# A fused transformer block on one core: normalisation and modulation move off GpSimd, one transposition in place of two, and the order of work made anew

## The chip, the core and the metric

The kernel runs on 1 core of one Trainium2 chip. A core has TensorE (PE: matrix products into PSUM, PEld is its weight load), VectorE (DVE), ScalarE (ACT), GpSimd (POOL) and SyncE (SP, which here issues nearly all DMAs). Each engine runs its own instruction queue in order, and the queues meet at semaphores. The metric is the device time of one execution in microseconds (us); the runs of the kernel before are three.

## What is computed

One block of a transformer in bf16, for a sequence of 2048 rows of width 640:

```python
mod = (_silu(c) @ w_mod).reshape(c.shape[0], 6, 1, -1)   # sa, ca, ga, sb, cb, gb
h = _layernorm(x, axis=-1) * (1 + ca) + sa
x = x + ga * _A_ref(h, A_wqkv, A_wo)      # attention, 32 heads of 20; key within the 256 rows up to the query
h = _layernorm(x, axis=-1) * (1 + cb) + sb
x = x + gb * _B_ref(h, B_w_gate, B_w_up, B_w_down)   # (sigmoid(h Wg) * (h Wu)) Wd, inner width 1536
```

## The kernel before

**Tiling.** The 2048 rows are 8 chunks (`a` = 0 to 7) of 256, each of two blocks of 128. For a chunk the kernel does in turn:

- `ln1` (from line 803): loads x, takes statistics (`ln_stats`, from line 737) and normalises in place; then turns the rows into columns, `hT`, and modulates. Chunks 0 and 1 turn on PE (`pe_transposes`, the evacuation from PSUM modulates, lines 799 and 800). The later ones turn by a DMA transposition (line 770) and are modulated in place (`modulate`, lines 778 and 779).
- `qkv`: products of 5 x 320 columns into PSUM, evacuated by DVE or ACT (lines 825 and 826) into `stg` for Q and K, which are then turned, and into `V`.
- `score_set` and `burst`: 6 sets of scores for each half of the heads (3 in chunk 0), 90 in all. A set fills four banks of PSUM, of which there is one buffer (`S`). ACT takes the exponential (line 937, 1.876 us), GpSimd masks the edges (lines 945 and 947), and PE sums values over a half's sets into two neighbouring banks of `M`.
- `norm`: DVE turns those two banks in blocks of 32 (line 988), takes the reciprocal of the sums (line 993), divides (line 995) and turns back (line 997). Two DMAs by way of a DRAM buffer, `doc`, bring the result into `oT`.
- `outproj`: products with wo, the first residual on DVE (line 1051), statistics, normalisation, DMA transposition and modulation into `h2T`.
- `mlp`: six pairs of gate and up products, tanh on ACT (line 1091), the glu product on DVE (line 1093), then the products with wd and the second residual (line 1112), and the DMA out.

**The normalisation.** For each of two blocks DVE takes two `bn_stats` (line 744) and an aggregation (line 746). GpSimd adds epsilon (line 749) and takes the power -1/2 (line 751), and one product per block makes minus mean times that (line 755). A normalisation is then a product and a sum (line 760), on DVE or on GpSimd. `XHE` names the engines that may take it, `MOE` those that may take a modulation.

**The prologue.** The modulation vector is made from silu(c) and three slabs of w_mod, which lie for that time where wd, wu and `hh` come later. PE multiplies each 128-row piece of the first slab as it lands (`modA`, `mA` is read out at line 732), with idle products between them (`fill`, line 653, and `warm`, line 642). The gates are folded into wo (line 1136) and wd (line 1077), a piece at a time on DVE.

**What sets the order.** No order is written out. `Prog.schedule` (from line 149) is a list planner: every operation has engines that may run it, a duration, a latency to its readers and a priority, and is placed on the engine that can start it first; among those that could start within a small window the priority decides. `PRI` shifts the priority of each kind of operation in each chunk by a number found outside the code. `port=True` marks DVE operations that the planner starts only when GpSimd is done, and the reverse. The order of each engine's queue, SP's too, is fixed by this when the program is built. Large weights (`bulk`) go through `chain`: a load may start when the one `DEEP` places back has landed.

```python
def chain():
    return [bulk[-DEEP]] if len(bulk) >= DEEP else front
```

The planner's `PACE0` and `PACE` give a score set an earliest time; `PE_EPS` is the window for PE.

Of the kernel before, what the change touches and what calls it, by code (L numbers as in the profile page):

```python
# [394 lines left out]
def c_pe(n):  # L395
# [3 lines left out]
PE_EPS = 0.141  # L399
PRI = {  # L400
    "amodu2": 9.3, "amodu3": -8.2, "amodu4": -88.6, "amodu5": -20, "amodu6": 43, "amodu7": 9, "apow0": 48.2,
    "apow1": 20.4, "apow2": 13.1, "apow3": -3.2, "apow4": -9, "apow5": 57.1, "apow6": 6.3, "apow7": 148.9,
    "astats0": -115.9, "astats2": -2.3, "astats3": -6.5, "astats4": 11.9, "astats5": -40.2, "astats6": -7.2,
    "atr2": -17, "atr3": -9.7, "atr4": 39.6, "atr5": 21.5, "atr6": 44.6, "atr7": 42.7, "axh0": 0.8, "axh1": 19.7,
    "axh2": 156.9, "axh3": 2.9, "axh5": -22.8, "axh6": 9.3, "axh7": -54.4, "bmodu0": 126.1, "bmodu1": 40.4,
    "bmodu2": 3.2, "bmodu3": 8.1, "bmodu4": -27.5, "bmodu5": 29.2, "bmodu6": -38.8, "bmodu7": 2.3, "bpow0": -12.3,
    "bpow1": -25.8, "bpow2": -3.6, "bpow3": 2.6, "bpow4": 23.5, "bpow5": -91.8, "bpow6": -2.4, "bpow7": -41.3,
    "bstats0": -27.1, "bstats1": -13.4, "bstats2": 9.8, "bstats3": 7, "bstats4": 2.4, "bstats5": -202.3,
    "bstats6": -1.7, "bstats7": -4.9, "btr0": -21.8, "btr1": -6.8, "btr2": 2.5, "btr3": 47.8, "btr4": 12.3,
    "btr5": -8.3, "btr6": 13.4, "btr7": 2.1, "bxh0": 1.1, "bxh1": -22.1, "bxh2": -2.1, "bxh3": 9.8, "bxh4": 21.6,  # L410
    "bxh6": -16.9, "bxh7": 12, "divide_0": 82.2, "divide_1": -4.7, "divide_2": 15.7, "divide_3": 13.6,
    "divide_4": 10.2, "divide_5": 10.5, "divide_6": 54.8, "down0": 67.2, "down1": 78, "down2": -3.1, "down3": 350.9,
    "down4": 114.6, "down6": 212.6, "down7": 13.6, "evqk0": 52.1, "evqk1": -14.4, "evqk2": 9.4, "evqk3": 13.1,
    "evqk4": 219.1, "evqk5": 50.7, "evqk6": 92.4, "evqk7": 34.6, "evqt0": 12.1, "evqt1": 160.3, "evv0": 3.4,
    "evv1": -5.6, "evv2": -3.9, "evv3": -0.9, "evv4": -6.5, "evv5": -28.9, "evv6": 6.9, "evv7": -3.5, "exp0": 43.9,
    "exp1": -25.4, "exp2": 156.2, "exp3": -15, "exp4": -34.1, "exp5": -28.7, "exp6": 24.3, "exp7": -25.4,
    "glu_0": 6.1, "glu_1": 21.7, "glu_2": 35.5, "glu_3": -16, "glu_4": -47.7, "glu_5": -9.6, "glu_6": -16.2,
    "glu_7": -15.9, "hTe0": -48.9, "hTe1": 0.2, "mask0": 96.8, "mask1": 2.7, "mask2": 33.7, "mask3": -16.3,
    "mask4": 141.5, "mask5": -12, "mask6": 92.1, "mask7": -13.4, "mlpg0": -25, "mlpg1": -24.5, "mlpg2": -24,
    "mlpu0": -25, "mlpu1": -24.5, "mlpu2": -24, "modb": -1, "modc": -0.8, "n_ow_0": -23.2, "n_ow_1": -17.7,  # L420
    "n_ow_2": -11.1, "n_ow_3": -61.2, "n_ow_4": -53.5, "n_ow_6": -3.1, "n_ow_7": -25.8, "oT_0": 33.6, "oT_1": -1.6,
    "oT_2": 14.5, "oT_3": -3.8, "oT_4": 55.9, "oT_6": -0.9, "oT_7": -3.3, "out": 6.8, "projk0": 4.5, "projk1": 12,
    "projk2": 394, "projk3": 157.7, "projk4": 21.4, "projk5": 189, "projk6": 15, "projk7": 7.2, "projq0": -62.7,
    "projq1": -34.6, "projq2": 51.7, "projq3": 33, "projq4": -15, "projq5": -10.5, "projq6": 468.1, "projq7": -7.6,
    "projv0": -30.9, "projv1": 19.1, "projv2": 152.9, "projv3": -2.2, "projv4": 60.2, "projv5": 41.1,
    "projv6": 285.1, "projv7": 183.7, "ptr0": -566.3, "ptr1": -245.2, "pv0": 18.7, "pv1": -2.9, "pv2": -12.3,
    "pv3": 4.1, "pv4": -11.6, "pv5": -18.8, "pv6": -88.2, "pv7": 104.2, "qkt2": 213.9, "qkt3": -6.3, "qkt4": 56.1,
    "qkt5": 18.6, "qkt6": 1.3, "qkt7": 5.8, "qtr0": -59.2, "qtr1": -6.6, "recip_0": 77.8, "recip_1": -10.5,
    "recip_2": 1.6, "recip_3": -88.1, "recip_4": 54.1, "recip_5": -1.7, "recip_6": 22.9, "recip_7": 10.1,
    "res1_0": 2.2, "res1_1": -17.7, "res1_2": -17.2, "res1_3": -20.4, "res1_4": 7, "res1_5": -126.9, "res1_6": -1.7,  # L430
    "res1_7": 45.3, "res2_0": 1.1, "res2_1": -11.9, "res2_2": -31.5, "res2_3": 51.8, "res2_4": 56.6, "res2_5": 0.1,
    "res2_6": -6.3, "res2_7": 58.7, "score0": -340, "score1": 16.4, "score2": -33.9, "score4": -104.9, "score5": -3,
    "score6": 7.3, "score7": -39.7, "tanh_0": -42.8, "tanh_1": -15.8, "tanh_2": 2.7, "tanh_3": -21.7,
    "tanh_4": -19.1, "tanh_5": -8.3, "tanh_6": -10.9, "tanh_7": -37.8, "tr1_0": 4.7, "tr1_1": 6.4, "tr1_2": 25.6,
    "tr1_3": -54, "tr1_4": 33.5, "tr1_5": 26.4, "tr1_6": -24.5, "tr2_0": 18.5, "tr2_1": -10.4, "tr2_3": -15.8,
    "tr2_4": -48.9, "tr2_5": 3.9, "tr2_7": -18.1, "wd": 0.6, "wds": -30.7, "wg": 27.5, "wm1": 26.4, "wm2": 15.6,
    "wo": -3.8, "wo0": 118.2, "wo1": 11.2, "wo2": 256.4, "wo3": 110.2, "wo4": 70, "wo5": 62.6, "wo6": -58.9,
    "wo7": 84.2, "wos": 7.1, "wu": -18.6, "x10": 1524.7, "x11": 1508.2, "x12": 1434.7, "x13": 1422.4, "x14": 1683.5,
    "x15": 1773.4, "x4": 1288, "x5": 929.8, "x6": 122, "x7": 26.3, "x8": 1341.3, "x9": 1354.8, "y0": -7.1,
    "y1": -20.9, "y10": -20.8, "y11": -5.7, "y12": -76.7, "y13": -41.2, "y14": -33.8, "y15": -8, "y2": 14.6,  # L440
    "y3": -5.6, "y4": -2.6, "y5": -11, "y6": -0.7, "y7": 42.2, "y8": -54.6, "y9": -32.1,
}
TR1 = 2
NPH = 2
NPQ = 2
DEEP = 4
MW = 64
PACE0 = 80.17
PACE = -6.665
AFTER = 0  # L450
LEAD = 2
FILL = 2
# [7 lines left out]
XHE = ('dve', 'pool')  # L460
MOE = ("dve", "act", "pool")


def build(nc, A_x, A_wqkv, A_wo, B_x, B_w_gate, B_w_up, B_w_down, c, w_mod, out, S=2048):
# [50 lines left out]
    p_st = sbpool("st", 3, [128, 34], F32)  # L515
# [51 lines left out]
    def load_x(pool, b, prio, tmin=0.0, eng="sp"):  # L567
        t = Tile(pool, f"{pool.name}_{b}")
        dma(lambda: t.ap[:], lambda: x_flat[b * 128:(b + 1) * 128, :], 0.47, writes=[t.r()], prio=prio, tmin=tmin, tag=f"x{b}" if pool is p_x0 else f"y{b}",
            eng=eng, lat=-0.7 if b > 3 else -0.4 if b < 2 else -1.0)  # L570
        return t
# [8 lines left out]
    def load_wm(i, kt, prio, tmin=0.0):  # L580
        if i:
            raise AssertionError
        return dma(lambda: wm_ap[i][:, kt, :], lambda: wm_src[:, kt, i * 1280:(i + 1) * 1280], 1.1, writes=[Rm[i][kt]], prio=prio, tmin=tmin, tag=f"wm{i}",
                   lat=-0.7)
# [15 lines left out]
    def load_w3(k, prio, halves):  # L600
# [6 lines left out]
        if k == "wk" and BQ != "sp":  # L607
            front.append(o)

    x0 = {}  # L610
    x0[0], x0[1] = load_x(p_x0, 0, 0), load_x(p_x0, 1, 0.1)
    for kt in range(NDT):
        load_wm(0, kt, 0.2 + 0.01 * kt)
    load_w3("wq", 0.30, True)
# [580 lines left out]
```

## Time and profile before

| | us |
|---|---|
| runs | 344.87, 343.16, 343.44 (median 343.44) |
| profiled execution | 344.87, its span 343.1, mean granted clock 0.995 |
| exponentials on ACT (line 937) | 168.8 in 90 |
| masks on GpSimd (lines 945, 947) | 78.8 and 68.1 |
| modulation on DVE (line 779) | 8.0 in 13 (hT) and 6.8 in 18 (h2T) |
| modulation on ACT (line 778) | 6.0 in 11 (hT) and 9.3 in 17 (h2T) |
| modulation on GpSimd (line 779) | 3.7 in 6 (hT) and 2.7 in 5 (h2T) |

A row of the profile's groups gives the line, the engine, the operation, what is written and read with its shape, the count, then busy time and mean duration in ns of one, then the engine's idle time just ahead of these instructions and who ended it. In rows of stretches each engine has its busy time and its number of instructions, then the granted clock, the DMA engines' busy share and the rate. PE's busy time counts products whose ends are modelled, so a full stretch may still hold short losses.

### The profile page before, as it was taken

The page shows a single profiled execution, that of the slowest core. Times are in us where ns is not written, and L with a number is a line of the kernel's source. Part 1 is how long each engine was busy: PE and PEld are TensorE (multiplying, and loading weights), DVE is VectorE, ACT ScalarE, POOL GpSimd, SP SyncE. Part 2 cuts the span into 40 slices and gives each one's busy share as a digit, 9 for nine tenths or more (in the row PEclk, how much of TensorE's full clock was granted, in tenths as well). Part 3 has the DMA queues.
Part 4 walks back from the last instruction along what each step waited for, and adds up shares of the span by engine and source line. Part 5 has one row for each costly group of instructions (what it writes and reads, how often), then busy time and mean ns, then how long its engine had stood idle before and what let it go on. Part 6 is the DMA issues. An engine that isn't in the chain of part 4 may idle for free.

```text
span 343.1 us, 10138 instructions
## 1 busy us (share of the span) xinstructions
PE 328.2 (96%) x4142; PEld 232.3 (68%) x4142; DVE 220.6 (64%) x440; ACT 232.2 (68%) x224; POOL 185.4 (54%) x285
## 2 busy tenths in 40 slices
PE   8889699989979999999999999999999999999997
PEld 2557365645756577766668767766676788887885
DVE  5378889498899964636784744558754654637333
ACT  1587669887966879878988877886888672120220
POOL 5044656668864876656797456559947471001000
PEclk9999899999999999999999999999999999999999
DMA  7999926799990391022763093004231211210301
GB/s 227 371 313 313 382 86 121 159 175 171 237 235 10 76 160 44 16 84 72 168 105 70 21 147 97 3 22 72 44 38 42 76 39 40 79 42 10 109 0 39
DMA packets 71688, 38.73 MB, mean 113 GB/s; under 512 B 46682, under 2 KB 68442, under 8 KB 71642
## 3 DMA queue, kind: packets, MB, share of 16 engines
q1 hardware_dynamic: 71632, 38.09, 45.3%
q8 instruction: 32, 0.52, 0.6%
q14 instruction: 14, 0.11, 0.1%
q10 hardware_dynamic: 10, 0.00, 0.0%
HBM read 21.96 MB, written 5.24 MB: 79 GB/s over the span
## 4 chain that ended last, share of the span: by engine, by line
PE 75%; DVE 9%; DMA 5%; SPq 3%; issue 2%; ACT 2%; POOL 2%; DVEq 0%; ACTq 0%
PE M L661 62%; PE S L662 7%; PE M L662 6%; SPq L536 3%; ACT E L937 2%; DMA wv<-in_A_wqkv_dram 2%; DVE wd L1077 2%; DMA wd<-in_B_w_down_dram 2%; DVE hT L779 2%; DMA hT<-x 1%; DVE x L1051 1%; DVE st L744 1%; POOL E L945 1%; POOL E L947 1%; DVE Tn L995 1%
## 5 line engine op out<-in xcount | busy, mean ns | idle before, releaser
L937 ACT ACTIVATE E<-S 128x2048 bf16<-128x2048 f32 x90 | 168.8, 1876 | 34.8 <-PE S L662 34.0
L945 POOL TENSOR_SCALAR_AFFINE_SELECT E<-E 128x512 bf16<-128x512 bf16 (+2 forms) x90 | 78.8, 877 | 79.5 <-ACT E L937 78.1
L947 POOL TENSOR_SCALAR_AFFINE_SELECT E<-E 128x512 bf16<-128x512 bf16 (+1 forms) x84 | 68.1, 812 | 0.0
L661 PE MATMUL M<-h2T,wg 128*128 128x256 bf16 x480 | 62.7, 273 | 2.0 <-DVE hh L1093 1.9
L661 PE MATMUL M<-h2T,wu 128*128 128x256 bf16 x480 | 64.4, 273 | 0.0
L1093 DVE SCALAR_TENSOR_TENSOR hh<-sig,M 128x512 bf16<-128x512 f32 x48 | 32.7, 681 | 47.9 <-PE M L661 33.1
L661 PE MATMUL M<-wd,hh 128*128 128x320 bf16 (+2 forms) x396 | 56.1, 295 | 0.0
L661 PEld LDWEIGHTS M<-h2T,wg 128*128 128x128 bf16 x480 | 45.3, 98 | 10.9 <-issue 2.2
L661 PEld LDWEIGHTS M<-h2T,wu 128*128 128x128 bf16 x480 | 45.2, 98 | 8.6 <-issue 2.7
L1091 ACT ACTIVATE sig<-M 128x512 f32<-128x512 f32 x48 | 28.5, 594 | 31.7 <-PE M L661 28.8
L661 PEld LDWEIGHTS M<-wd,hh 128*128 128x128 bf16 x396 | 37.0, 98 | 15.2 <-issue 1.5
L662 PE MATMUL S<-QT,KT 20*128 20x256 bf16 (+1 forms) x960 | 35.9, 245 | 1.6 <-ACT E L937 1.5
L988 DVE STREAM_TRANSPOSE T<-M 128x512 f32<-128x512 f32 x32 | 21.1, 696 | 20.2 <-PE M L662 20.1
L744 DVE BATCH_NORM_STATS2 st<-x 128x6 f32<-128x320 bf16 x64 | 28.3, 477 | 4.1 <-DMA x<-in_A_x_dram 3.8
L749 POOL TENSOR_SCALAR st<-st 128x2 f32<-128x2 f32 x16 | 4.8, 304 | 47.0 <-DVE st L746 46.4
L662 PEld LDWEIGHTS S<-QT,KT 20*128 20x128 bf16 x960 | 14.1, 92 | 22.3 <-ACT E L937 18.1
L1112 DVE TENSOR_TENSOR x<-M,x 128x320 bf16<-128x320 f32 (+2 forms) x33 | 15.6, 474 | 19.7 <-PE M L661 19.6
L661 PE MATMUL M<-wv,hT 128*128 128x320 bf16 x160 | 27.1, 314 | 1.2 <-DMA wv<-in_A_wqkv_dram 0.9
L661 PE MATMUL M<-wq,hT 128*128 128x320 bf16 x160 | 24.7, 299 | 0.6 <-DVE V L826 0.3
L661 PE MATMUL M<-wo,oT 128*128 128x320 bf16 x160 | 24.6, 300 | 0.5 <-DVE x L1051 0.5
L661 PE MATMUL M<-wk,hT 128*128 128x320 bf16 x160 | 24.8, 300 | 0.1
L662 PE MATMUL M<-E,V 128*32 128x256 bf16 (+1 forms) x960 | 22.7, 246 | 1.5 <-POOL E L947 0.9
(78 smaller groups left out, 334.2 us busy)
## 6 DMA issues: line engine op xcount, KB each, us to landing
x<-in_A_x_dram SPq DMA_DIRECT2D x32, 160.0 KB, 2.4
doc<-On SPq DMA_DIRECT2D x64, 40.0 KB
out_dram<-x SPq DMA_DIRECT2D x15, 160.0 KB
wg<-in_B_w_gate_dram SPq DMA_DIRECT2D x5, 384.0 KB
wu<-in_B_w_up_dram SPq DMA_DIRECT2D x5, 384.0 KB
wd<-in_B_w_down_dram SPq DMA_DIRECT2D x4, 480.0 KB
wd<-in_w_mod_dram SPq DMA_DIRECT2D x5, 320.0 KB, 4.9
wu<-in_w_mod_dram SPq DMA_DIRECT2D x5, 320.0 KB
```

The costliest lines, as they stand in the source:

```text
L536: return e.dma_start(dst(), src())
L661: return e.matmul(o, l, r, start=st, stop=sp, skip_group_check=True)
L662: return e.matmul(o, l, r, start=st, stop=sp, tile_position=tp, skip_group_check=True)
L744: A("dve", lambda e, g, bi=bi, j=j: e.bn_stats(v(bi * 12 + j * 6, 6), src[bi].ap[:, j * 320:(j + 1) * 320]), 0.48, reads=[src[bi].r()], wr ...
L779: return e.tensor_scalar(ap, ap, sc[:, dt:dt + 1], sh[:, dt:dt + 1], op0=ALU.mult, op1=ALU.add)
L937: A("act", lambda e, eng: e.activation(E.ap[:], Sp.ap[:], ACT.Exp, scale=SM_SCALE), 1.876, reads=[Sp.r()], writes=[E.r()], prio=3, tag=f"e ...
L945: return e.affine_select(ap, ap, pattern=[[0, ap.shape[1]], [1, 128]], compare_op=ALU.is_ge, fill=0.0, base=0, channel_multiplier=-1)
L947: return e.affine_select(ap, ap, pattern=[[0, ap.shape[1]], [-1, 128]], compare_op=ALU.is_ge, fill=0.0, base=-1, channel_multiplier=1)
L988: A("dve", lambda e, g, h=h: e.transpose(T1.ap[:, 512 * h:512 * h + 512], X[h].ap), 0.694, reads=[X[h].r()], writes=[T1.r(h)], prio=3.5, t ...
L1091: A("act", lambda e, g, pg=pg, sg=sg: e.activation(sg.ap[:], pg.ap[:], ACT.Tanh, scale=0.5), c_act(512), reads=[pg.r()], writes=[sg.r()], ...
L1093: A("dve", lambda e, g, pu=pu, sg=sg, f0=f0: e.scalar_tensor_tensor(out=hh.ap[:, f0:f0 + 2, :], in0=sg.ap[:].rearrange("p (a b) -> p a b", ...
L1112: A("dve", lambda e, g, ps=ps, bi=bi, c0=c0, n=n: e.tensor_tensor(x1[bi].ap[:, c0:c0 + n], ps.ap[:, 0:n], x1[bi].ap[:, c0:c0 + n], op=ALU. ...
```

## The change

- `TR1` 2 to 1: one transposition of 1024 columns over both banks of `M` in place of two of 512. The code path was there.
- `XHE` without GpSimd: every normalisation on DVE, as subtraction of the mean and a product; the two small products of line 755 are gone.
- `MOE` without GpSimd: modulation on DVE or ACT.
- The first two x blocks are loaded from ACT's queue, in place of the front of SP's.
- silu(c) is spread to 128 columns by one copy in place of two of 64.
- `DEEP` 4 to 3; nine idle products of two in the warm-up in place of five; `FILL` 2 to 1.
- The planner's constants: durations and latencies of DMAs and of DVE operations, `PE_EPS`, `PACE0`, `PACE` and nearly all of `PRI` (left out below). With them the order on all engines is another one. DVE's queue has 441 instructions (440 before), ACT's 229 with two more DMA issues among them (224) and GpSimd's 232 (285).

In that order all five pieces of the first slab are multiplied ahead of the transposes of x, the scalings of wo are spread over more of DVE's queue, and those of wd stand in groups of 3, 4, 1, 2, 1 and 1 between other work. SP's queue has one piece more of the second slab behind wv. The last scores stand, as before, ahead of two chunks of MLP.

```diff
-PE_EPS = 0.141
+PE_EPS = 0.116
...
-TR1 = 2
+TR1 = 1
...
-DEEP = 4
+DEEP = 3
...
-PACE0 = 80.17
-PACE = -6.665
+PACE0 = -178.4
+PACE = -4.513
...
-FILL = 2
+FILL = 1
...
-XHE = ('dve', 'pool')
-MOE = ("dve", "act", "pool")
+XHE = ("dve",)
+MOE = ("dve", "act")
...
-    p_st = sbpool("st", 3, [128, 34], F32)
+    p_st = sbpool("st", 3, [128, 32], F32)
...
-        dma(lambda: t.ap[:], lambda: x_flat[b * 128:(b + 1) * 128, :], 0.47, writes=[t.r()], prio=prio, tmin=tmin, tag=f"x{b}" if pool is p_x0 else f"y{b}",
-            eng=eng, lat=-0.7 if b > 3 else -0.4 if b < 2 else -1.0)
+        dma(lambda: t.ap[:], lambda: x_flat[b * 128:(b + 1) * 128, :], 0.47 if b > 1 else 0.9, writes=[t.r()], prio=prio, tmin=tmin, tag=f"x{b}" if pool is p_x0 else f"y{b}",
+            eng=eng, lat=0.05 if b > 1 else 1.2)
...
-        return dma(lambda: wm_ap[i][:, kt, :], lambda: wm_src[:, kt, i * 1280:(i + 1) * 1280], 1.1, writes=[Rm[i][kt]], prio=prio, tmin=tmin, tag=f"wm{i}",
-                   lat=-0.7)
+        return dma(lambda: wm_ap[i][:, kt, :], lambda: wm_src[:, kt, i * 1280:(i + 1) * 1280], (1.12 - 0.06 * kt if kt < 4 else 1.2), writes=[Rm[i][kt]],
+                   prio=prio, tmin=tmin, tag=f"wm{i}")
...
-                            prio=prio + 0.01 * k, tag=tag, lat={"wm1": -1.0, "wm2": -0.6}.get(tag, 0.05), extra=list(extra) + chain(), eng=BQ,
+                            prio=prio + 0.01 * k, tag=tag, extra=list(extra) + chain(), eng=BQ,
...
-                    (2.35 if hi - lo == 640 else 0.95 if i == 0 else 1.35), lat=-1.0, writes=[R_w3[k][lo // 320]] if halves else R_w3[k], prio=prio, tag=k)
+                    (2.35 if hi - lo == 640 else 1.28), writes=[R_w3[k][lo // 320]] if halves else R_w3[k], prio=prio, tag=k)
...
-    x0[0], x0[1] = load_x(p_x0, 0, 0), load_x(p_x0, 1, 0.1)
+    x0[0], x0[1] = load_x(p_x0, 0, 0, eng="act"), load_x(p_x0, 1, 0, eng="act")
...
-    A("dve", lambda e, g: e.tensor_copy(silubc[:, :, 0:MW], siluc[:].unsqueeze(2).to_broadcast([128, NDT, MW])), 0.45,
-      reads=[R_siluc], writes=[R_silubc], prio=-1)
-    R_silub2 = R("silub2")
-    A("dve", lambda e, g: e.tensor_copy(silubc[:, :, MW:128], siluc[:].unsqueeze(2).to_broadcast([128, NDT, 128 - MW])), 0.45,
-      reads=[R_siluc], writes=[R_silub2], prio=6)
+    A("dve", lambda e, g: e.tensor_copy(silubc[:], siluc[:].unsqueeze(2).to_broadcast([128, NDT, 128])), 0.8,
+      reads=[R_siluc], writes=[R_silubc], prio=0)
...
-    for i in range(5):
+    for i in range(9):
...
-            ops.append(pe_chain(ps, 320, pairs, [[Rm[i][kt], R_silubc, R_silub2] for kt in range(NDT)], prio, "modb"))
+            ops.append(pe_chain(ps, 320, pairs, [[Rm[i][kt], R_silubc] for kt in range(NDT)], prio, "modb"))
...
-            if "pool" in XHE:
-                A("pool", lambda e, g, bi=bi: e.tensor_scalar(st.ap[:, 32 + bi:33 + bi], v(24 + 2 * bi, 1), v(30 + bi, 1), -1.0,
-                                                              op0=ALU.mult, op1=ALU.mult), 0.25,
-                  reads=[st.r("r"), st.r(("m", bi))], writes=[st.r(("n", bi))], prio=1, tag=f"{ln}pow{a}")
-
-                def xh(e, g, bi=bi):
-                    return e.tensor_scalar(dst[bi].ap[:], src[bi].ap[:], v(30 + bi, 1), v(32 + bi, 1), op0=ALU.mult, op1=ALU.add)
-            else:
-                def xh(e, g, bi=bi):
-                    return e.tensor_scalar(dst[bi].ap[:], src[bi].ap[:], v(24 + 2 * bi, 1), v(30 + bi, 1), op0=ALU.subtract,
-                                           op1=ALU.mult)
-            A(XHE, xh, {"dve": 0.5, "pool": 1.2}, port=True,
-              reads=[src[bi].r(), st.r("r"), st.r(("m", bi))] + ([st.r(("n", bi))] if "pool" in XHE else []), writes=[dst[bi].r()], prio=prio - 0.5, tag=f"{ln}xh{a}")
+            A(XHE, lambda e, g, bi=bi: e.tensor_scalar(dst[bi].ap[:], src[bi].ap[:], v(24 + 2 * bi, 1), v(30 + bi, 1),
+                                                       op0=ALU.subtract, op1=ALU.mult), {"dve": 0.44, "pool": 0.95}, port=True,
+              reads=[src[bi].r(), st.r("r"), st.r(("m", bi))], writes=[dst[bi].r()], prio=prio - 0.5, tag=f"{ln}xh{a}")
...
-        return A("sp", fn, dur, reads=reads, writes=writes, prio=prio, work=work, tag=tag, lat=-0.7)
+        return A("sp", fn, dur, reads=reads, writes=writes, prio=prio, work=work, tag=tag)
...
-            A(MOE, mo, {"dve": 0.4, "act": 0.59, "pool": 0.6}, port=True, reads=[dst.r(("t", bi)) for bi in range(2)] + Rmod, writes=[dst.r(dt)],prio=prio, tag=f"{ln}modu{a}")
+            A(MOE, mo, {"dve": 0.34, "act": 0.59, "pool": 0.55}, port=True, reads=[dst.r(("t", bi)) for bi in range(2)] + Rmod, writes=[dst.r(dt)],prio=prio, tag=f"{ln}modu{a}")
...
-                fills.append(fill(FILL, [o]))
+                fills.append(fill(2 * FILL, [o]))
...
-          0.92, port=True, reads=[T1.r(0), T1.r(1), Dr.r()], writes=[Tn.r()], prio=4, tag=f"divide_{a}")
+          0.82, port=True, reads=[T1.r(0), T1.r(1), Dr.r()], writes=[Tn.r()], prio=4, tag=f"divide_{a}")
...
-                    reads=[On.r()], writes=[Rj], prio=1, tag=f"n_ow_{a}", lat=-0.6)
+                    reads=[On.r()], writes=[Rj], prio=1, tag=f"n_ow_{a}")
...
-                0.22 * (t1 - t0), reads=R_doc[0] + (R_doc[1] if q else []), writes=[oT.r(q)], prio=1.5, tag=f"oT_{a}", lat=0.6)
+                0.22 * (t1 - t0), reads=R_doc[0] + (R_doc[1] if q else []), writes=[oT.r(q)], prio=1.5, tag=f"oT_{a}")
```

## The prediction

> **What bounds the kernel now.** I read the busy shares first, then the slices in time, then the PE waits, then the stretches where PE idles, then the groups for prices.
>
> The page's busy shares:
>
> ```profile
> span 343.1 us, 10138 instructions
> PE 328.2 (96%) x4142; PEld 232.3 (68%) x4142; DVE 220.6 (64%) x440; ACT 232.2 (68%) x224; POOL 185.4 (54%) x285
> ```
>
> PE is the bound: only 343.1 - 328.2 = 14.9 us of the span are not PE. The edit takes no projection, score, value or MLP product away, so it can gain at most those 14.9 us, and it loses whatever new PE idleness it makes. By stretches of 10 us (stretch, then busy PE, PEld, DVE, ACT, POOL, then clock, DMA share, GB/s):
>
> ```profile
> 10.00:20.00 10.00, 8.26 (x90) 5.62 (x88) 4.83 (x13) 6.27 (x13) 2.32 (x5) 1.00 1.06 363
> 20.00:30.00 10.00, 9.73 (x112) 6.99 (x108) 7.91 (x21) 8.83 (x14) 3.64 (x6) 1.00 0.97 339
> 30.00:40.00 10.00, 7.24 (x129) 4.68 (x117) 9.29 (x19) 7.45 (x7) 7.09 (x8) 1.00 1.08 324
> ...
> 70.00:80.00 10.00, 8.39 (x90) 5.05 (x89) 9.81 (x23) 8.95 (x11) 6.77 (x11) 1.00 0.89 211
> ...
> 100.00:110.00 10.00, 7.45 (x134) 5.37 (x135) 9.31 (x20) 4.81 (x5) 4.69 (x9) 1.00 0.27 85
> ...
> 160.00:170.00 10.00, 10.00 (x170) 6.57 (x162) 6.14 (x15) 8.81 (x9) 6.88 (x12) 1.00 0.71 159
> ```
>
> Three stages. Up to 30 us the DMA share is about 1: loads set the pace. From 30 to 120 us PE is busy 81.4 of 90 us (8.6 idle) and DVE 78.4 of 90 (0.87; sums of the nine stretches). The three stretches where PE idles most are three of those where DVE is above 0.92. From 120 us PE shows next to no idle time until the end. The PE's waits name the engine (waiter, releaser, total, times, longest):
>
> ```profile
> PE M L661 <- DVE stg L826: 2.9, 2, 2.7
> PE M L661 <- DVE hh L1093: 1.9, 1, 1.9
> ```
>
> The first is at 38.94 us: the evacuation of a K half stands on DVE behind one modulation that took 1.85 us and one scaling of wo that took 1.39 us; their kinds' shortest are 0.33 and 0.49. GpSimd runs three masks, 4.35 us, in just that time. The second is at 102.96 us: a glu product stands behind nine scalings of wd. So DVE in its first third is the second resource, and the change is about DVE. Prices:
>
> ```profile
> L988 DVE STREAM_TRANSPOSE T<-M 128x512 f32<-128x512 f32 x32 | 21.1, 696 | 20.2 <-PE M L662 20.1
> L997 DVE STREAM_TRANSPOSE On<-Tn 128x1024 bf16<-128x1024 bf16 x16 | 19.8, 1236 | 0.2
> L760 DVE TENSOR_SCALAR x<-x,st 128x640 bf16<-128x640 bf16 x22 | 11.4, 542 | 2.7 <-POOL st L755 2.5
> L760 POOL TENSOR_SCALAR x<-x,st 128x640 bf16<-128x640 bf16 x10 | 8.7, 868 | 0.2 <-POOL st L755 0.2
> L755 POOL TENSOR_SCALAR st<-st 128x1 f32<-128x1 f32 x32 | 8.2, 271 | 1.6
> L779 DVE TENSOR_SCALAR hT<-hT,mA 128x256 bf16<-128x256 bf16 x13 | 8.0, 650 | 0.2 <-DMA hT<-x 0.2
> ```
>
> **The change, part by part.**
>
> *Normalisation and modulation.* The instruction order of the changed kernel has 32 normalisations on DVE (22 now) and 41 modulations (31 now), 29 on ACT (28), none on GpSimd; two more evacuations of hT from PSUM stand on DVE and four others fewer. DVE gains 10 x 0.542 + 10 x 0.477 (14.8 us for 31) + 2 x 0.535 = 11.3 us and loses 2 x 0.483 + 0.485 + 0.69 = 2.1. GpSimd loses 8.7 + 8.2 + 6.4 = 23.3 us; it has 46% idle time and its masks end late at one place only, so that frees little. What counts is where it falls. Of the normalisations on GpSimd four start between 30 and 120 us (46.12, 79.75, 107.22, 116.65 us), and four modulations (34.50, 58.98, 87.19, 90.41). There DVE gets 4 x 0.542 + 4 x 0.650 = 4.8 us more. Ends: 0, if all falls into the 90 - 78.4 = 11.6 us that DVE has free, and 4.8 us, if each stands in front of something that PE waits for. I take 0.87 x 4.8 = 4.2 us: the queue runs in order and is occupied 87% of the time, and two of the three worst PE gaps are such cases. The rest falls after 120 us, where DVE is free a third of the time; nothing.
>
> The order also foresees less of this than the trace shows. The code plans 0.34 us for a modulation, 0.44 for a normalisation, 0.82 for the division. The trace has 0.477, 0.542 and 0.946 (15.1 us for 16). That is 41 x 0.137 + 32 x 0.102 + 16 x 0.126 = 10.9 us of DVE not in the plan; with the constants before (0.40, 0.50, 0.92) it was 31 x 0.077 + 22 x 0.042 + 16 x 0.026 = 3.7. It is the reason to stay near the upper end; it is no term of its own.
>
> *Shorter statistics chain.* Two products of 271 ns go on GpSimd, and a normalisation on the chain falls from 868 to 542 ns. The chain of waits passes this once (78.1 to 80.6 us, the last statistics before the first MLP): 2 x 0.27 + 0.33 = 0.9 us. Ends 0 and 0.9 (PE lost a wait of 0.9 us on a GpSimd mask just after it); I take 0.9.
>
> *One transposition.* Two of 512 columns take 1.31 us back to back (timeline, several times); one of 1024 columns is not in the trace, except in bf16 from SBUF (1.236 us). Saved: 0.07 x 16 = 1.2 us of DVE at most. The first PSUM bank comes free some 0.5 us later, but PE has two others and the next scores; DVE waited 20.1 us in total for PE before these, not the reverse. Ends: -1.2 and, as PE's waits name this transposition nowhere, a burst or two, +1.0 us; I take 0.
>
> *Prologue.* The first two x loads leave SP's queue (0.40 + 0.42 us of issue) for ACT's. The modulation weights are issued 0.9 us earlier, and their last product now stands ahead of the transposes of x instead of behind them. PE idled 0.5 us before the fourth and 0.8 us soon after the fifth, so 0 to 1.3 us earlier start of the projections. SP's queue then waits for landings three loads back instead of four. When wv landed, at 18.56 us, before had 3360 KB to go until the third modulation slab (its last load, issued at 27.05 us, takes 4.3 us, thus 31.3 us): 264 KB per us. PE started on that slab at 31.52 us, straight after it, so this landing sets the pace. The new queue has one more 320 KB load behind wv: 320 / 264 = 1.2 us later. Ends: -1.3 (the early start is kept) and +4.2 (the chain of loads is the limit, and 3 in flight instead of 4 stretch 12.7 us by a third). I take +1.2. The early start is worth nothing as long as PE arrives at the slab before its data.
>
> [...]
>
> *The rest.* The copy of silu(c) in one piece of 640 columns (two of 0.36 and 0.34 now) delays the first product by about 0.3 us, but that one waits for its weights anyway; nothing. More idle matmuls in the warm-up stand in idle time, and the clock reads 1.00 after it. The scalings of wd are now spread between glu products instead of nine in a row: that could take the 1.9 us away, but the same loads land late and the queue is in order, so I count nothing and put it into a rival. After 120 us the order is another one, with the same sets between the same amounts of other products; the trace has no price for it: -1 to +2 us, 0 taken. The tail is the same three pieces.
>
> **Sum.** 4.2 - 0.9 + 0 + 1.2 = +4.5 us. The profiled execution took 344.87 us (span 343.1 and 1.8 around it) and becomes 349.4. It is 1.43 us above the median of the runs, 343.44; the prediction for the median is 343.44 + 4.5 = **347.9 us**.
>
> **Rivals.**
>
> 1. *Faster: the new order frees DVE exactly where PE waits.* Place: the K evacuation at 38.9 us and the glu at 103.0 us. The order has wo's scalings split by other work and wd's in groups of 3, 4, 1, 2, 1, 1 between glu products. If both stalls go and the added work fits into DVE's free time, the prologue stays as it is, and the statistics gain stands: 343.44 - 2.7 - 0.9 = 339.8 with the first alone, 337.9 with both. It decides if DVE's added 4.8 us go into its 11.6 free ones. For it: GpSimd does less beside DVE, and normalisations on DVE have a median of 447 ns, far under the mean. Against it: the single ones reach 1357 ns beside masks, and there are more of them. 0.19.
>
> 2. *All hidden.* PE's 328.2 us are untouched and the 4.8 us vanish in slack: 343.4, within 1.7. Before has 8.6 us of idle PE in the stage, which speaks against so exact a cover. 0.17.
>
> 3. *Slower by much:* three loads in flight starve the prologue (+4.2 in place of +1.2) and a second DVE stall of 2.7 us appears where the order is planned too tight: 347.9 + 3.0 + 2.7 = 353.6. 0.20.
>
> That the edit misses its target is excluded: the instruction order shows all normalisations on DVE and 16 transpositions of 1024 columns.
>
> **Chances.** Forecast (345.2 to 350) 0.44; the three rivals 0.19, 0.17, 0.20. About 0.5%, 1.7 us, is what a measurement of this kernel can tell from no change. Faster by more 0.19, within it 0.17, slower 0.64. The range reaches from the first stall of rival 1 to rival 3: 339.8 to 353.6. The forecast's own range is 345.2 to 350.
>
> **What would show it.** Right: PE idle time between 30 and 120 us above 8.6 us, ended by DVE (evacuations, modulations, glu); DVE near 228.6 us in total, GpSimd near 162; PE's first product of the third slab after 32 us; 120 to 320 us full. Wrong: PE idle below 8.6 us there, or a new PE idle stretch after 120 us, which nothing in this sum pays for.

## The result, and the profile after

The changed kernel takes 340.03 us (median of 339.42 to 340.71), the kernel before 343.80 beside it; the ratio is 0.9888, interval 0.9855 to 0.9921. A second series gave 0.9920 (0.9888 to 0.9953). The prediction was 347.9 us: the sign is wrong. The medians here and below take in every execution, while the ratios leave out those that took over 1.5% more than the fastest of the same kernel, among them one of the changed kernel of 822.42 us at a clock of 1.00, whose cause is open.

The profiled execution took 340.71 us. Its page begins as before's did, with the span and the busy shares:

```profile
span 339.0 us, 10076 instructions
PE 327.9 (97%) x4146; PEld 232.4 (69%) x4146; DVE 220.2 (65%) x441; ACT 233.2 (69%) x227; POOL 159.0 (47%) x232
```

PE's busy time is the same within 0.3 us, so 3.8 of the 4.1 us of span are standstill of PE that is gone (14.9 us before, 11.1 now). GpSimd is at 159.0 (foreseen 162). DVE is at 220.2 where 228.6 was foreseen: with 10 normalisations and 10 modulations more it is no busier than before (220.6). The same stretches as shown for before (stretch, PE, PEld, DVE, ACT, POOL, clock, DMA share, GB/s):

```profile
10.00:20.00 10.00, 9.79 (x106) 6.79 (x105) 6.27 (x16) 8.00 (x15) 0.93 (x2) 1.00 0.97 337
20.00:30.00 10.00, 8.66 (x117) 5.18 (x117) 8.06 (x23) 8.16 (x9) 6.21 (x7) 1.00 0.89 296
30.00:40.00 10.00, 7.93 (x125) 5.30 (x118) 7.19 (x13) 6.84 (x9) 4.91 (x4) 1.00 0.97 245
...
70.00:80.00 10.00, 9.18 (x149) 5.83 (x142) 9.45 (x27) 8.32 (x10) 7.99 (x14) 1.00 0.79 144
...
100.00:110.00 10.00, 10.00 (x144) 6.83 (x133) 9.64 (x22) 7.30 (x5) 4.58 (x6) 1.00 0.01 2
...
160.00:170.00 10.00, 10.00 (x157) 6.48 (x155) 8.14 (x20) 8.70 (x8) 7.63 (x12) 1.00 0.38 101
```

From 100 to 110 us PE is full although DVE is still busy 96% of the time: a busy engine is no stall as long as the right instruction comes first in its queue. Over 30 to 120 us PE is busy 85.04 us (81.38 before), DVE 74.24 (78.36), GpSimd 50.94 (60.70), and the granted clock reads 1.00 (0.98). PE's waits, whole span:

```profile
PE M L657 <- DVE stg L812: 1.9, 3, 1.2
PE M L657 <- DMA hh<-in_w_mod_dram: 1.4, 3, 1.0
PE M L658 <- DVE gbc L705: 1.4, 1, 1.4
```

The waits of 2.7 and 1.9 us in one piece are gone; the longest now is 1.4. The prices of DVE's groups moved too:

```profile
L977 DVE STREAM_TRANSPOSE T<-M 128x1024 f32<-128x1024 f32 x16 | 20.0, 1248 | 16.8 <-PE M L658 16.6
L750 DVE TENSOR_SCALAR x<-x,st 128x640 bf16<-128x640 bf16 x32 | 17.2, 569 | 4.0 <-POOL st L747 3.9
L1063 DVE TENSOR_TENSOR wd<-wd,gbc 128x640 bf16<-128x640 bf16 x12 | 6.5, 565 | 0.2
L765 DVE TENSOR_SCALAR hT<-hT,mA 128x256 bf16<-128x256 bf16 x19 | 6.4, 394 | 0.0
```

Ten more normalisations cost 5.8 us (17.2 less 11.4; 5.4 were priced). But a modulation of hT fell from 650 to 394 ns, a scaling of wd from 761 to 565, a division from 946 to 889: together 19 x 0.256 + 12 x 0.196 + 16 x 0.057 = 8.1 us that the prediction's prices, taken from the old trace, did not have.

**Where the time came from.** I set the two traces side by side at equal amounts of PE work done (lag of the changed kernel, an estimate worked out from the starts of PE's products; the kernels do the products in different orders, so it is good to some 0.6 us, and is less exact where a wait begins):

| place in the kernel before, us | lag, us | what lies there |
|---|---|---|
| 18.8 | -1.7 | earlier start; before waits 0.9 for wv |
| 31.8 | +1.4 | third modulation slab |
| 35.2 | +3.4 | values wait for the gate evacuation (1.4 wait) |
| 43.3 | -1.0 | before's K evacuation stall and what follows it |
| 71 | -0.4 | |
| 84 | -2.0 | before's waits for exponentials, x and a mask |
| 106 | -4.3 | before's glu stall behind nine wd scalings |
| end | -4.5 | |

The prologue's early 1.7 us are lost again and more. Most of the gain is made where rival 1 put it: 4.4 us between 35.2 and 43.3 us, 2.3 between 84 and 106, and 1.6 besides between 71 and 84. Of the 4.4 us, 2.0 only make good what the changed kernel has just lost at its own wait (1.4 to 3.4), so some 2.4 stay. The 4.4 are more than the stall of 2.7 itself, because TensorE's clock fell behind it. Rows of the kernel before:

```profile
36.00:38.00 2.00, 0.27 (x2) 0.00 (x0) 2.00 (x2) 1.63 (x1) 2.00 (x2) 1.00 1.03 400
38.00:40.00 2.00, 0.97 (x22) 0.56 (x22) 2.00 (x5) 0.60 (x1) 1.44 (x2) 1.00 1.05 375
40.00:42.00 2.00, 2.00 (x24) 1.09 (x13) 1.52 (x4) 1.75 (x1) 0.00 (x0) 0.55 1.05 411
42.00:44.00 2.00, 2.00 (x11) 1.16 (x10) 1.57 (x5) 0.36 (x2) 1.81 (x1) 0.59 0.86 318
```

PE is busy in the last two rows, at 0.55 and 0.59 of its clock: 2 x 0.45 + 2 x 0.41 = 1.7 us of delay that no row of idle time shows.

### The profile page after: what moved, and what is told of

The parts are those of the page before. It is cut to its first block, busy times and chain, and to the rows that moved or that the text cites. A ratio compares the mean times of both kernels' runs of the same rounds, so it can differ in the third digit from the quotient of the medians.

```text
span 339.0 us, 10076 instructions
## 1 busy us (share of the span) xinstructions
PE 327.9 (97%) x4146; PEld 232.4 (69%) x4146; DVE 220.2 (65%) x441; ACT 233.2 (69%) x227; POOL 159.0 (47%) x232
## 4 chain that ended last, share of the span: by engine, by line
PE 62%; DVE 0%; issue 0%
PE M L657 52%; PE S L658 5%; PE M L658 4%; DVE x L1098 0%
## 5 line engine op out<-in xcount | busy, mean ns | idle before, releaser
L931 POOL TENSOR_SCALAR_AFFINE_SELECT E<-E 128x512 bf16<-128x512 bf16 (+2 forms) x90 | 78.0, 866 | 104.3 <-ACT E L923 103.3
L933 POOL TENSOR_SCALAR_AFFINE_SELECT E<-E 128x512 bf16<-128x512 bf16 (+1 forms) x84 | 67.0, 798 | 0.0
L657 PE MATMUL M<-h2T,wu 128*128 128x256 bf16 x480 | 63.0, 273 | 0.0
L977 DVE STREAM_TRANSPOSE T<-M 128x1024 f32<-128x1024 f32 x16 | 20.0, 1248 | 16.8 <-PE M L658 16.6
L658 PEld LDWEIGHTS S<-QT,KT 20*128 20x128 bf16 x960 | 14.1, 92 | 20.9 <-ACT E L923 14.9
L657 PE MATMUL M<-wk,hT 128*128 128x320 bf16 x160 | 26.3, 300 | 1.7 <-DVE stg L812 1.2
L657 PE MATMUL M<-wv,hT 128*128 128x320 bf16 x160 | 25.1, 300 | 0.0
L658 PEld LDWEIGHTS M<-E,V 128*32 128x32 bf16 x960 | 20.0, 97 | 6.2 <-issue 4.3
```

Of the source, the lines that this page charges most:

```text
L657: return e.matmul(o, l, r, start=st, stop=sp, skip_group_check=True)
L658: return e.matmul(o, l, r, start=st, stop=sp, tile_position=tp, skip_group_check=True)
L931: return e.affine_select(ap, ap, pattern=[[0, ap.shape[1]], [1, 128]], compare_op=ALU.is_ge, fill=0.0, base=0, channel_multiplier=-1)
L933: return e.affine_select(ap, ap, pattern=[[0, ap.shape[1]], [-1, 128]], compare_op=ALU.is_ge, fill=0.0, base=-1, channel_multiplier=1)
L977: A("dve", lambda e, g: e.transpose(T1.ap[:], Mall[:, X[0].slot:X[0].slot + 2, :].rearrange("p a c -> p (a c)")), 1.23, reads=[X[0].r(), X ...
```

## The experiments

All were compared with runs of the kernel before beside them (medians 343.7 to 344.4). In most kernels the planner's order is kept as it is, and single operations are exchanged, moved or dropped after planning; diffs show that step. `place(P, ...)` puts the named operations of DVE's queue, in that order, at the places that they held. A tag is the operation's kind and chunk, the number its turn.

| kernel | median, us | ratio to before, interval |
|---|---|---|
| after_again: the changed kernel | 341.28 | 0.9920, 0.9888 to 0.9953 |
| b_spread: before, wd scalings spread | 343.13 | 0.9973, 0.9938 to 1.0008 |
| a_bunch: after, wd scalings in a row | 346.19 | 1.0037, 1.0004 to 1.0071 |
| b_engines: before's order, new engine split | 346.30 | 1.0041, 1.0010 to 1.0073 |
| a_engines: new order, before's engine split | 345.92 | 1.0038, 1.0009 to 1.0067 |
| b_kfirst: before, K evacuation first | 344.97 | 1.0019, 0.9979 to 1.0059 |
| b_nostall: before, both stalls cut up | 343.36 | 0.9958, 0.9923 to 0.9993 |
| a_ladder: after, six standstills added | 358.43 | 1.0355, 1.0264 to 1.0446 |
| a_xh: after, 10 normalisations on GpSimd | 344.41 | 1.0008, 0.9985 to 1.0032 |
| a_mod: after, 11 modulations on GpSimd | 341.65 | 0.9914, 0.9883 to 0.9946 |
| a_tr2: after, two transpositions | 340.07 | 0.9888, 0.9845 to 0.9932 |
| a_deep4: after, four loads in flight | 339.55 | 0.9883, 0.9839 to 0.9928 |
| a_swaps: after, two exchanges on DVE | 341.38 | 0.9949, 0.9915 to 0.9982 |
| b_replan: before, new split, planned anew | 346.75 | 1.0024, 0.9989 to 1.0060 |
| a_replan: after, old split, planned anew | 391.03 | 1.1281, 1.1217 to 1.1344 |
| a_best: after, four in flight, two exchanges | 338.50 | 0.9823, 0.9791 to 0.9855 |

I began with two theories. *Order*: the gain is made by the remade queues, above all by wd's scalings; the engine moves are worth little. *Engines*: it is made by what left GpSimd.

**b_spread** and **a_bunch** take the wd scalings apart and together.

```diff
     P.schedule()
+    place(P, [glu_0/0, wds/0, glu_0/1, wds/1, wds/3, wds/2, wds/4, wds/6, glu_0/2, wds/5, wds/7, wds/9,
+              wds/8, glu_0/3, wds/10, wds/11, glu_0/4, glu_0/5])          # b_spread
+    place(P, [glu_0/0, wds/0, wds/1, wds/3, glu_0/1, wds/2, wds/4, wds/6, wds/5, wds/7, wds/8, wds/9,
+              wds/10, wds/11, glu_0/2, glu_0/3, glu_0/4, glu_0/5])        # a_bunch
     P.emit()
```

> The kernel before with one thing changed: of the wd scalings on VectorE, which in before stand nine in a row ahead of the third product of tanh and up projection of MLP 0 (95.3 to 102.3 us), only as many stand ahead of each product as the down projection behind it needs; every engine keeps its work. Theory order (the gain of the changed kernel is made by the remade order, between 70 and 108 us, where the wd scalings no longer stand in a row ahead of a product that TensorE waits for): TensorE's 1.9 us stall at 103 us and the 0.85 us behind it go, the time is 2.0 to 2.9 us below before, 340.9 to 341.8. Theory engines (the gain is made by moving GpSimd's normalisations and modulations to VectorE and ScalarE): 0, 343.4 to 344.

> The changed kernel with the nine wd scalings that it has spread between the products of MLP 0 put in one row behind the second product, as before has them; every engine keeps its work. Theory order: TensorE waits for the third product as in before, 2 to 4 us more than the changed kernel, 342 to 344. Theory engines: the scalings are shorter than before's (565 against 761 ns a piece) and wd is loaded 3.5 us earlier, so VectorE has them done in time; 0 to 0.7 more, 340 to 340.7.

b_spread: 0.27% less, 0.9 us, with an interval that reaches zero. In its trace the glu stall's place gains 2.0 us, but 1.5 are given back 2 us later, in a wait of 2.2 us for a later glu product. a_bunch: 1.0037 against 0.9920, 4.0 us more than the changed kernel, at the upper end for the order theory. PE's waits between 88 and 112 us, and DVE's row:

```profile
PE M L718 <- DVE hh L1140: 3.2, 2, 2.1
```

```profile
93.78 5.69 DVE L1124 TENSOR_TENSOR wd<-wd,gbc 128x640 bf16<-128x640 bf16 x7 [0.42 <-DMA wd<-in_B_w_down_dram]
99.39 1.28 DVE L1140 SCALAR_TENSOR_TENSOR hh<-sig,M 128x512 bf16<-128x512 f32 x2
```

Seven scalings, 5.69 us, stand ahead of two glu products; PE waits 3.2 us, and the clock behind it reads 0.50 for the stretch from 102 to 104 us. So this piece of the order is needed for the gain.

**b_engines** and **a_engines** exchange the split under a fixed order; the transposition goes with it (one of 1024 columns in b_engines, two of 512 in a_engines).

```diff
     P.schedule()
+    for key in POOLED:            # 10 normalisations, 11 modulations
+        move(P, n[key], "dve")    # b_engines; "pool" in a_engines
+    for o in NEG:                 # the products of mean and power
+        drop(P, o)                # b_engines; put back in a_engines
     P.emit()
```

> Before's order of work on every queue with the engine split of the changed kernel: the 10 normalisations and 11 modulations that GpSimd has in before go to VectorE at the same places, the products of mean and power are gone, one transposition of 1024 columns stands for two of 512. Theory order: no gain without the new order, 343.8, from 0 to 3 us more if VectorE's added 8 to 10 us of work show (the prediction's term of 4.2 us is a part of this theory). Theory engines: the gain of the changed kernel comes with it, 340 to 341.

> The changed kernel's order of work with before's engine split: 10 normalisations and 11 modulations back on GpSimd, the products of mean and power with them, two transpositions of 512 columns for one of 1024. Theory order: the gain stays, 340.0, from 0 to 1 us more. Theory engines: the gain is lost, about 343.8.

Neither theory is enough. The new split in the old order is 0.41% slower than before (1.4 us, 0.3 to 2.5), as the order theory allowed and the engines theory did not; the old split in the new order is 1.18% slower than the changed kernel, 4.1 us, which is slower than before as well, and there the order theory falls. Between 30 and 120 us, where the prediction charged the moved work, PE is busier in b_engines than in before (rows of before, b_engines and the changed kernel):

```profile
30.00:120.00 90.00, 81.38 (x1074) 53.11 (x1062) 78.36 (x155) 71.03 (x69) 60.70 (x84) 0.98 0.71 169
30.00:120.00 90.00, 83.67 (x1092) 54.54 (x1085) 80.94 (x161) 73.45 (x71) 53.26 (x67) 0.98 0.73 171
30.00:120.00 90.00, 85.04 (x1159) 56.19 (x1152) 74.24 (x152) 74.71 (x78) 50.94 (x69) 1.00 0.76 171
```

So PE's idle time there is 8.6, 6.3 and 5.0 us. By the lag, b_engines is still some 2 us ahead of before at 168 us; then PE waits 2.3 us for a transposition on DVE and runs at half clock:

```profile
168.00:170.00 2.00, 0.61 (x11) 0.21 (x3) 2.00 (x5) 2.00 (x2) 0.92 (x2) 1.00 0.77 181
170.00:172.00 2.00, 1.13 (x5) 0.68 (x6) 1.46 (x2) 0.22 (x1) 1.71 (x2) 0.60 0.43 85
172.00:174.00 2.00, 2.00 (x10) 1.16 (x9) 1.54 (x4) 0.24 (x1) 0.42 (x1) 0.54 0.00 0
```

In a_engines PE waits for GpSimd, 3.2 us for masks and 2.4 for h2T, 4.0 of the two behind 120 us, where the prediction saw nothing to pay.

**a_xh**, **a_mod** and **a_tr2** take a_engines apart: the same edit with the normalisations and their products alone, with the modulations alone, and two `transpose` calls of 512 columns for each one of 1024.

```diff
-e.transpose(T1.ap[:], Mall[:, X[0].slot:X[0].slot + 2, :].rearrange("p a c -> p (a c)"))
+e.transpose(T1.ap[:, 0:512], X[0].ap)
+e.transpose(T1.ap[:, 512:1024], X[1].ap)
```

> The changed kernel's order with 10 normalisations back on GpSimd, and the products of mean and power with them; modulations and the transposition stay as changed. With the modulations on GpSimd as well it took 4.6 us more, and TensorE waited 3.2 us for GpSimd's masks and 2.4 for its modulations. If GpSimd's queue is what counts, these 8.7 + 8.2 of the 23.3 us hold the masks up: 1.5 to 3.5 us more than the changed kernel, 342.5 to 345. If only the modulations on GpSimd cost: 0 to 0.7 more.

> The changed kernel's order with 11 modulations back on GpSimd; normalisations and transposition as changed. With normalisations and modulations back it was 4.6 us more than the changed kernel, with the normalisations alone 3.1. If the costs add: 1.0 to 2.0 more, 342 to 343.5, and TensorE waits for h2T on GpSimd. If they are one and the same overload of GpSimd's queue: 0 to 0.5 more.

> The changed kernel with two transpositions of 512 columns in place of each one of 1024, back to back at the same place; the rest as changed. The prediction counted this part as nothing, with ends of -1.2 and +1.0. Traces: 2 x 0.694 against 1.248 us, 16 times, is 2.2 us more of VectorE's time. If that time were on the path of TensorE: 1 to 2.2 us more than the changed kernel. If it is covered: 0, within 0.5.

The normalisations cost 0.88%, 3.0 us: GpSimd's queue is what counts. The modulations cost nothing that is seen (0.9914). The 1.1 us that are missing to a_engines' 4.1 are within the intervals; whether they appear only when both are there is not shown. The transpositions cost nothing (0.9888). Of DVE's time they take less than the 2.2 us of the expectation: two of 694 ns overlap and take 1.31 us back to back, against 1.25, 1.0 us for 16. PE's waits in a_xh, and GpSimd's row behind one of them:

```profile
PE M L712 <- POOL E L990: 3.1, 3, 1.3
```

```profile
216.60 0.50 POOL L807 TENSOR_SCALAR st<-st 128x1 f32<-128x1 f32 x2
217.08 1.72 POOL L804 TENSOR_SCALAR x<-x,st 128x640 bf16<-128x640 bf16 x2
218.76 1.10 POOL L988 TENSOR_SCALAR_AFFINE_SELECT E<-E 128x1024 bf16<-128x1024 bf16 x1
```

Two products and two normalisations, 2.2 us, stand ahead of a mask; in the changed kernel that mask starts at 216.51. The values of the burst need the mask, and PE waits 1.3 us for it at 220 us.

**b_kfirst** and **b_nostall** test the stall at 38.9 us.

```diff
     P.schedule()
+    place(P, [evqk1/3, amodu3/4, wos/4])                                        # b_kfirst
+    place(P, [evqk1/2, evqk1/3, wos/4, gbc/0, evqt1/2, gbc/1, amodu3/4])        # b_nostall, and b_spread's
     P.emit()
```

> The kernel before with one evacuation moved up on VectorE: the K half that TensorE waits 2.67 us for at 38.9 us is evacuated ahead of the modulation (1.85 us) and the scaling of wo (1.39 us) that stand in front of it; every engine keeps its work. Theory clock (the standstill of 2.67 us also halves TensorE's granted clock, which reads 0.55 and 0.59 in the two stretches from 40 to 44 us, so it costs about 1.7 us on top of itself): 3.2 to 4.2 us less than before. Rival, stall alone (the low clock has some other cause and stays): 1.7 to 2.3 us less, and the clock between 40 and 44 us still reads 0.5 to 0.6. Theory engines gives this stall no part in the gain, but foresees the same time.

> The kernel before with both exchanges on VectorE's queue: the wd scalings spread between the products of MLP 0, and at 35 to 40 us the K evacuation first, then the scaling of wo, then the gate evacuations, and the long modulation (1.85 us) behind them. Every engine keeps its work. The standstill of 2.67 us becomes two of 0.6 and about 1.4, and that of 1.9 us goes. Theory clock: without a standstill over 2 us most executions keep the full clock (mean 1.00 where before reads 0.99 or 0.995), and the time is 0.7 + 1.7 + 1 to 2 less, 340 to 341.5, as fast as the changed kernel without any of its engine moves. Rival (waits only move on, as in the exchange of the K evacuation alone): 343 to 344.5 and the clock at 0.99 to 0.995.

Neither theory foresaw b_kfirst: no gain (1.0019). Its PE waits say why:

```profile
PE M L722 <- DVE gbc L770: 2.1, 1, 2.1
...
PE M L722 <- DVE stg L887: 0.8, 2, 0.6
```

The K evacuation comes 2.4 us earlier, and PE stands at the next thing on DVE, the gate evacuation behind the wo scaling: 0.59 + 2.12 = 2.71 us, before 2.67. DVE has the same work to do in that stretch in whatever order. The clock stayed at 1.00 there in this trace, but fell elsewhere: behind 2.5 us of waiting for a glu product at 101 us (0.57 and 0.58 from 102 to 106), and behind waits around 72 us (0.50 from 76 to 78). b_nostall gains 0.42% (1.4 us): its stall at 37 us is in three pieces of 0.6, 1.0 and 0.8 us by the waits, and the clock falls even so (0.50 in each microsecond from 40 to 43). So it is not the one long standstill alone that lowers it. The time and the clock are those that the rival foresaw (343 to 344.5 us, 0.99 to 0.995): the waits move on.

**a_ladder** asks that directly, in a quiet part.

```diff
     P.schedule()
+    for key, cols in STEPS:
+        k = P.op("dve", memset of cols columns of a free buffer, tag="idle")
+        k.deps = [product ahead of key on PE]
+        n[key].deps.append(k)
     P.emit()
```

> The changed kernel with six standstills of TensorE added on purpose behind 290 us, some 6.5 us apart, where nothing else stops it and hardly a DMA runs: ahead of a product stands a wait for a VectorE fill of chosen length. In order about 1.6, 2.6, 2.0, 3.2, 2.3 and 1.8 us, 13.5 in sum. Theory clock (a standstill over some 2.2 us lowers the granted clock to one half for about 3.4 us behind it, which costs 1.7 us more; the traces so far have it after 2.28, 2.3, 2.5 and 2.67 us, not after 1.9 and 2.12): the clock falls behind the second, fourth and fifth and behind no other, and the time is 13.5 + 3 x 1.7 = 18.6 us above the changed kernel, about 360. Rival (the low clock belongs to the loads and the busy engines of the first 110 us, not to the standstill): the clock stays at 1.00 behind all six, 13.5 us more, about 355.

PE waited 1.38, 2.38, 1.78, 2.98, 2.08 and 1.58 us, 12.2 in sum. The clock fell behind 2.38 and behind no other, not even 2.98:

```profile
305.00:307.00 2.00, 1.13 (x11) 1.02 (x12) 1.35 (x2) 0.00 (x0) 0.00 (x0) 0.99 0.00 0
307.00:309.00 2.00, 2.00 (x12) 1.40 (x10) 0.00 (x0) 1.57 (x3) 0.00 (x0) 0.50 0.04 8
309.00:311.00 2.00, 2.00 (x14) 1.48 (x13) 1.46 (x4) 0.00 (x0) 0.00 (x0) 0.66 0.00 0
324.00:326.00 2.00, 0.29 (x3) 0.27 (x4) 2.00 (x2) 0.00 (x0) 0.00 (x0) 1.00 0.00 0
326.00:328.00 2.00, 2.00 (x20) 1.79 (x19) 0.00 (x0) 0.60 (x1) 0.00 (x0) 1.00 0.23 82
```

The theory of a fixed length falls, and so does its rival: no load and no busy engine but DVE with its fill is near (DMA share, ACT and GpSimd 0.00 in the row from 305 to 307 us). The three executions took 353.91, 358.43 and 362.18 us at mean clocks of 0.995, 0.990 and 0.981: the same program, and by these clocks a different number of low phases (one, two and four, an estimate from 1.7 us of loss for each).

A low phase lasts 3.41 us in before (the clock reads 0.50 from 40.22 to 43.63 us) and 3.4 in a_ladder (0.98, 0.50, 0.50, 0.50 and 0.81 in the microseconds from 306 to 311); at half clock that is 1.7 us of loss. Such phases came behind single waits of 2.3 (b_engines, behind 168 us) to 2.90 us (b_spread, at 38 us), and behind clusters of shorter ones, in b_nostall of 0.6, 1.0 and 0.8 us. So the length of a wait alone does not decide in these traces: the one of 2.98 us left the clock at 1.00. What decides is not shown.

**a_deep4**, **a_swaps**, **a_best** try what is left.

```diff
     P.schedule()
+    for i, o in enumerate(bulk):           # a_deep4, a_best: wait for the load four places back
+        if i >= 3:
+            o.deps.remove(bulk[i - 3])
+            o.deps += [bulk[i - 4]] if i >= 4 else front
+    place(P, [wos/3, wos/4, gbc/0, gbc/1, axh3/0, axh3/1])                    # a_swaps
+    place(P, [evqk2/4, tr2_0/1])                                              # a_swaps
+    place(P, [wos/3, axh3/0, wos/4, gbc/0, gbc/1, axh3/1])                    # a_best
+    place(P, [recip_0/0, amodu2/1, amodu2/2, amodu2/4, evqt1/3, divide_0/0])  # a_best
     P.emit()
```

> The changed kernel as it is, as the reference on the chip of the runs beside it. All theories: 340.0 to 341.5, 0.986 to 0.992 of the kernel before.

> The changed kernel with the chain of large loads waiting for the landing four places back, as in before, in place of three; all queues keep their order. If three loads in flight hold back the third modulation slab (a bound of the prediction's prologue term), TensorE's waits of 1.4 us for hh fall below 0.5 and the time is 1 to 2.5 us less. Rival (the DMA engines are full either way, and the slab is late because one more load stands ahead of it): 0, within 0.5, and hh lands when it did.

> The changed kernel with two places on VectorE's queue exchanged: the two gate evacuations that the first values wait 1.36 us for at 38.6 us go ahead of two normalisations, and one Q evacuation, which TensorE waits 1.2 us for at 54 us, goes ahead of a transposition of 1.25 us. If what stands in front of an evacuation on VectorE's queue sets the time in this stage (theory order): 1.2 to 2.2 us less, 338 to 339. If such a wait only moves to the next one: 0 to 0.5 less.

> The changed kernel with the chain of large loads waiting four places back and with two evacuations moved up on VectorE: the gate evacuations ahead of the second normalisation at 37 us, and a K evacuation ahead of the division at 42 us. If these add up: 0.5 to 1.5 less than with the chain alone, 338 to 339. If the waits move on, as in the two exchanges tried before: 339.5 to 340.5.

after_again is the reference. a_deep4 is lower by 0.37%, 1.3 us, but the intervals overlap. PE's wait for hh is 1.3 us (1.4 and 0.9 in the two traces of the changed kernel), and the slab's products end 0.1 and 0.5 us earlier than in those: open. In a_swaps the wait of 1.4 us at the values is gone, but that for a K evacuation grows from 0.5 to 1.6; ahead of it DVE stands 0.96 us for a DMA transposition. No gain, the wait moves on. a_best, with that K evacuation moved up too, is at 0.9823, below both kernels; its interval, 0.9791 to 0.9855, ends where the changed kernel's first one begins. How much of it is the chain and how much the exchanges isn't told apart.

**b_replan** and **a_replan** let the planner make the order again.

```diff
-XHE = ('dve', 'pool')
-MOE = ("dve", "act", "pool")
+XHE = ("dve",)              # b_replan; the reverse, with the products, in a_replan
+MOE = ("dve", "act")
```

> The kernel before with one part of the change: normalisations on VectorE alone and modulations on VectorE and ScalarE, and the order planned again with all the planner's numbers as they were before (two transpositions, four loads in flight). With the same split in before's fixed order the time was 346.3. If freeing GpSimd pays by itself once an order fits it: 340 to 342. If the gain needs the numbers that were found for this split (joint theory): 344.5 to 350, and TensorE waits for VectorE more than before.

> The changed kernel with GpSimd allowed again for normalisations and modulations (with the products of mean and power), and the order planned again with all the changed numbers. If the order alone carries the gain: 340 to 342. Joint theory: the numbers fit one split only, 346 or more, and how much more is open, since the planner moves other work too.

b_replan is not faster than before (1.0024), and a_replan takes 391 us. The joint theory stands: the moves off GpSimd pay only in an order made for them, and that order only with the moves. Whether other numbers would make an order as good for the old split wasn't tried.

## Why the prediction was wrong

- **What bounds it**: right. PE's 328 us stayed; the change lives on its 14.9 us of standstill, now 11.1.
- **Normalisation and modulation, +4.2: the step that failed.** It charged 4.8 us of moved work with DVE's occupancy, 0.87, as if each moved instruction stood in front of PE with that chance. With the order left as it was, the whole move costs 1.4 us (b_engines), and not there: PE's idle time from 30 to 120 us falls from 8.6 to 6.3 us, and the loss comes behind 168 us, where the prediction put nothing. In the new order that idle time went from 8.6 to 5.0 us, below the 8.6 that the prediction named as the sign of being wrong. Occupancy says how often a new instruction delays the next one on its engine, not how often PE needs that one. And DVE did not get fuller: the other prices fell.
- **"That frees little" of GpSimd: wrong.** In the new order 10 normalisations and their products there cost 3.0 us (a_xh). GpSimd's idle half is of no use to a mask that stands behind a normalisation in its queue (in a_xh one starts at 218.76 us, in after_again at 216.51). The prediction saw the one late mask of 0.9 us and did not carry it over to the other chunks.
- **Statistics chain, -0.9**: not shown alone. The mask wait beside it is 0.5 us now.
- **One transposition, 0**: right (a_tr2); DVE saved 1.0 us of the 1.2 priced.
- **Prologue, +1.2**: right in size. PE is 1.4 us late at the end of the third slab, and the early start of 1.7 us is lost. How much of it is the three loads in flight stays open (a_deep4). That PE multiplies the slab's pieces as they land, from 27.5 us, was not foreseen, so the test "first product after 32 us" asked the wrong thing.
- **The wd scalings, "I count nothing": wrong.** a_bunch prices them at 4.0 us in the new order. The reason given against them, that the loads land late, holds in the old order (b_spread gains only 0.9 us); the new one issues three of wd's four loads 3.5 us earlier, at 84.98 in place of 88.45 us, which the prediction did not count on.
- **Behind 120 us, 0**: right for the change as a whole (-4.3 and -4.5 us of lag at 106 us and at the end), but only because order and split fit; a_engines loses most there, b_engines loses there what it had won.
- **Rival 1** named the places of the gain. Its price for the K stall, 2.7 us, lacked the clock, with which the stall cost 4.4 us, and the wait of 1.4 us that the changed kernel has there instead. The prologue, which it left as it was, lost more than 1 us. So it is in part luck that its 339.8 us lie beside the measured 340.03.

The clock also shows in the runs. Of the 96 executions of before that the comparisons of the four series use, 47 had a mean clock of 0.990 (mean time 344.7 us), 44 of 0.995 (343.8) and 5 of 1.00 (341.2); of the changed kernel's 14, 10 had 1.00 (340.6). So at full clock the two kernels are within some 0.6 us, and most of the difference of their medians goes with the number of low phases: one or two in before's executions, mostly none in the changed kernel's. This is a count, not a proof: an execution without low phases may also be one with shorter stalls.

## What to carry to other kernels

Price moved work by who waits behind it on the queue at that place, not by the engine's busy share; and count what becomes shorter on the engine that is emptied and on its neighbour. Where a planner's numbers were found for one split, neither the split nor the order can be priced alone: test both halves with the queues held fixed. Look at the granted clock in the rows behind TensorE's long waits, and behind clusters of shorter ones: here a wait of 2.67 us cost 1.7 us again, and three of 0.6, 1.0 and 0.8 us were followed by the low clock too.

## What the runs showed that I had not expected

- TensorE at 0.50 of its clock for about 3.4 us, some 1.7 us lost, behind waits of 2.1 (a_bunch, one of 1.1 beside it), 2.3 (b_engines), 2.38 (a_ladder), 2.5 (b_kfirst), 2.67 (before) and 2.90 us (b_spread, at 38 us), but not behind 1.9 (before), 2.08 (a_ladder), 2.12 (b_kfirst), 2.2 (b_spread) and 2.98 (a_ladder); in b_nostall it stands behind three of 0.6, 1.0 and 0.8.
- DVE's prices rise beside GpSimd: one scaling of wo took 2.29 us beside a mask of 2.10 us in the changed kernel, where the shortest takes 0.44. In the two main traces the 23 normalisations on DVE with no GpSimd instruction beside them took at most 447 ns, the others up to 1357. The glu products, which read PSUM, took at most 690 either way.
- A transposition of 1024 columns on DVE takes 1248 ns; two of 512 take 1.31 us back to back (696 ns each, overlapping).
